# 64-row matmul pairs in the first product of a top-2 expert kernel, with one operand copied to the upper partitions by a DMA

## The chip, the cores and the metric

The kernel runs on one core of one Trainium2 chip. The metric is the device time of one execution in microseconds (us), as the median of several runs. The engines are named as in the profile: PE is TensorE's matmul, PEld its weight load, DVE VectorE, ACT ScalarE, POOL GpSimd, and SP is SyncE, which here only issues DMAs. A "q" behind an engine's name (SPq) means its sequencer.

## What is computed

A causal convolution over the sequence with 7 taps (softmax of a weight per head) makes x of 28672 tokens with 192 columns. Each token goes to the best two of 8 experts, by noisy logits, and the two results are added with their gates:

```python
    logits = x @ w_gate
    noise_scale = np.log1p(np.exp(x @ w_noise))
    noisy_logits = logits + noise_scale * noise
    top2 = np.argpartition(-noisy_logits, 2, axis=1)[:, :2]
    ...
    for e in range(E):
        for k in range(2):
            mask = top2[:, k] == e
            ...
            h = np.maximum(x[mask] @ w1[e], 0.0)
            out[mask] += top2_w[mask, k, None] * (h @ w2[e])
```

D is 192, E is 8, F is 1024; all inputs and the output are float32.

## The kernel before

**Units and rows.** The tokens go through convolution and gating in 28 units of 1024 tokens. `conv` writes a unit's rows as float16 pairs into the tile `rb`: in 384 columns stand the high parts of x's columns 0 to 127, their low parts, and then, together in the third chunk of 128, the 64 high and the 64 low parts of x's columns 128 to 191. `gating(u)` begins by putting loads of noise and a DMA of zeros on SP, then eight DMA transposes of `rb` into `xT` (L475); its later parts compute the logits (L484, with matmuls on `xT`), the top two, the rank of each token (L541, L544) and the row of each token in its expert's region of `xs` in DRAM. POOL scatters the rows there (L570).

**Blocks.** The expert part runs over blocks: rounds of 256 rows (the first round 128), and in each round the experts 0 to 7. That is 232 blocks in order. `load_block` transposes a block's rows out of `xs` into the tile `bT` (L692, by SP; three buffers), with the 384 columns as three chunks of 128 partitions. So chunk 0 holds the high parts of columns 0 to 127, chunk 1 their low parts, and chunk 2 the last 64 columns' high parts on partitions 0 to 63 and their low parts on partitions 64 to 127. The weights are float16 pairs too; the last 64 rows of w1 lie twice, on the lower and on the upper partitions.

**The first product.** `mm1` does half of a block's 1024 hidden columns at a time: four groups `f` of 128 hidden columns into the tile `ph` (two banks, two groups in each), each by five matmuls of 128 rows (L658): weights high and low with chunk 0, weights high with chunk 1, and weights high and low with chunk 2. ACT (L661) and DVE (L662) then make the float16 pair `h` of the half. `mm2` does the second product of 48 matmuls for the block before (L672), ACT scales it (L675), and POOL adds it to the output in DRAM (L676).

**The order.** PE, DVE, ACT and SP execute in the order in which the program issues. Step n of the loop issues: the first half of block n's `mm1`; `prefetch(n + 2)`, which puts the load of block n + 2 on SP; `side.slot(0)`; `mm2` of block n - 1; the second half of block n's `mm1`; `side.slot(1)`. A slot issues pieces of the next units' convolution and gating, as many as a written budget of VectorE time allows, and with them their DMAs: x's load for the next unit (L179) and what `gating` puts on SP. The first units are done ahead of the blocks, in a written order. At the end a loop over overflow rows follows, whose number is computed on the chip.

**Weight scales.** Ahead of the blocks, `gram` (L268) multiplies each expert's weights with themselves, in bfloat16 with 128 columns: per expert 8 matmuls of 128 rows and 8 of 64 rows for w1, and 12 of 128 rows for w2, directly behind each other.

Of the kernel before, what the change touches and what calls it, by code (L numbers as in the profile page):

```python
# [10 lines left out]
F16 = mybir.dt.float16  # L11
# [8 lines left out]
P = 128  # L20
# [12 lines left out]
def kernel(  # L33
# [11 lines left out]
    nc = tc.nc  # L45
# [3 lines left out]
    E, _, F = w1.shape  # L49
# [6 lines left out]
    BIG = 2 * P  # L56
# [4 lines left out]
    rounds = [(0, P)] + [(P + mean * j, mean) for j in range(U)]  # L61
# [24 lines left out]
    start = tc.tile_pool(name="start", bufs=1)  # L86
    spool = start.__enter__()

    xs = dram.tile([E * REG, ROW], F16, name="xs")
# [105 lines left out]
    def parts(e, c):  # L195
        slots, n = ((slots1, 2 * e + c), (slots2, 2 * e + c - 2))[c // 2]
        w = slots[n].bitcast(F16).rearrange("p (a f) -> p a f", a=2)
        return slots[n + 1], w[:, 0], w[:, 1]

    def w1_part(e, c, lo, f):  # L200
        return parts(e, c)[1 + lo][:, f * P:(f + 1) * P]
# [392 lines left out]
    def load_meta(j):  # L594
        start, T = rounds[j]
        mt = ffn.tile([P, E, 2, 8], F32, name="mt", padded_shape=[P, E, 2, 8])
        for h in range(T // P):
            ld = nc.sync.dma_start(
                mt[:, :, h, :],
                dview(xsf, (start + h * P) * ROWF + 192, [[ROWF, P], [REG * ROWF, E], [1, 8]]))  # L600
            loads(ld, j)
        return mt

    def round_meta(j, mt):
        start, T = rounds[j]
        ids, ga = meta(mt, T // P, runs[:, ready[j] + 1, :], float(start))
        if j:
            unscale(ga, slice(0, E), T // P)
        return ids, ga
# [27 lines left out]
    def unscale(ga, es, nh):  # L637
        V.tensor_tensor(ga, ga, winv[:, es, None].to_broadcast([P, es.stop - es.start, nh]), op=OP.mult)
# [3 lines left out]
    def loads(ld, j):  # L642
        for u in scat:
            if u > ready[j]:
                tc.declare_no_dep(ld.ins, group=f"scat{u}", reason="rows behind the block")
            elif u not in waited:
                for s in scat[u]:
                    needs(ld, s)
        waited.update(range(ready[j] + 1))
        tc.add_to_no_dep_group("loads", ld.ins)  # L650

    def mm1(e, xT, T, half, hh, hl):
        nf = FC // 2
        ph = psum.tile([P, nf, BIG], F32, name="ph", bufs=2)
        for f in range(nf):
            seq = [(0, 0, 0), (1, 0, 0), (0, 0, 1), (0, 1, 2), (1, 1, 2)]
            for i, (lo, wc, c) in enumerate(seq):
                nc.tensor.matmul(ph[:, f, :T], w1_part(e, wc, lo, half * nf + f), xT[:, c, :T], start=(i == 0),  # L658
                                 stop=(i == len(seq) - 1))
        hs = slice(half * nf, (half + 1) * nf)  # L660
        halves.append(nc.scalar.activation(hh[:, hs, :T], ph[:, :, :T], AF.Relu))  # L661
        V.scalar_tensor_tensor(hl[:, hs, :T], ph[:, :, :T], 0.0, hh[:, hs, :T], op0=OP.max, op1=OP.subtract)  # L662

    def mm2(j, T, e, hh, hl, ids, gate):
        adds = []
        for h in range(T // P):
            ts = slice(h * P, (h + 1) * P)
            py = psum.tile([P, 512], F32, name="py", bufs=2)
            n = 0
            for f in range(FC):  # L670
                for a, lo in ((hh, 0), (hh, 1), (hl, 0)):
                    nc.tensor.matmul(py[:, :D], a[:, f, ts], w2_part(e, lo, f), start=(n == 0), stop=(n == 3 * FC - 1))  # L672
                    n += 1
            y = ffn.tile([P, D], F32, name="y", bufs=4)
            nc.scalar.activation(y, py[:, :D], AF.Copy, scale=gate[:, h:h + 1])  # L675
            a = nc.gpsimd.indirect_dma_start(  # L676
                out=out, out_offset=bass.IndirectOffsetOnAxis(ap=ids[:, h:h + 1], axis=0),
                in_=y, in_offset=None, compute_op=OP.add)
            for b in adds:
                tc.declare_no_dep(a.ins, b.ins, reason="one expert's rows differ")  # L680
            for u in zeroed:
                if u > ready[j]:
                    tc.declare_no_dep(a.ins, group=f"zeros{u}", reason="rows of tokens not among the block's")
            adds.append(a)
        for a in adds:
            tc.add_to_no_dep_group("adds", a.ins)

    def load_block(j, e):
        start, T = rounds[j]
        xT = ffn.tile([P, 3, BIG], F16, name="bT", bufs=3)  # L690
        r0 = e * REG + start
        ld = nc.sync.dma_start(xT[:, :, :T], xs[r0:r0 + T, 0:384], transpose=True)  # L692
        loads(ld, j)
        return xT


    HH = H // 2
# [44 lines left out]
    ffn = ctx.enter_context(tc.tile_pool(name="ffn", bufs=2))  # L742
# [91 lines left out]
    blocks = [(j, e) for j in range(len(rounds)) for e in range(E)]  # L834
    xTs, metas, mts = {}, {}, {}
# [3 lines left out]
    def prefetch(n):  # L839
        if n < len(blocks) and n not in xTs:  # L840
            j, e = blocks[n]
            side.until(ready[j])
            if e == 0:
                mts[j] = load_meta(j)
            xTs[n] = load_block(j, e)

    for n in range(AHEAD):
        prefetch(n)
    pend = None
    for n, (j, e) in enumerate(blocks):  # L850
        T = rounds[j][1]
        need = max(ready[min(i, len(rounds) - 1)] + j - i for i in range(j, j + 5))
        rate = RATES[min(max(side.gate_done - need, 0), 2)]
        if j not in metas:
            metas[j] = round_meta(j, mts.pop(j))
        ids, gate = metas[j]
        while prepared[0] < e:
            next(prep, None)
        if j == 0:
            unscale(gate[:, e:e + 1, :], slice(e, e + 1), T // P)  # L860
        xT = xTs.pop(n)
        h = ffn.tile([P, 2, FC, BIG], F16, name="h")
        mm1(e, xT, T, 0, h[:, 0], h[:, 1])
        prefetch(n + AHEAD)
        spent = 0.0
        if e == E - 1 and j + 1 < len(rounds):
            metas[j + 1] = round_meta(j + 1, mts.pop(j + 1))
            spent = 1.6
        side.slot(0, T, rate, spent)
        if pend:  # L870
            mm2(*pend)
        mm1(e, xT, T, 1, h[:, 0], h[:, 1])
        side.slot(1, T, rate)
        pend = (j, T, e, h[:, 0], h[:, 1], ids[:, e, :], gate[:, e, :])
# [13 lines left out]
    with tc.If(total > 0):  # L888
        ctr = small.tile([P, 1], F32, name="ctr")
        for e in range(E):  # L890
            nb = nc.values_load(noi[0:1, e:e + 1], engines=engines, min_val=0, max_val=N // P)
            V.memset(ctr, float(cap))
            with tc.For_i(0, nb, 1) as i:
                row = i * P + (e * REG + cap)
                xT = ffn.tile([P, 3, BIG], F16, name="bT", bufs=3)
                nc.sync.dma_start(xT[:, :, :P], xs[bass.ds(row, P), 0:384], transpose=True)
                mt = ffn.tile([P, 1, 1, 8], F32, name="mto")
                nc.sync.dma_start(mt[:, 0, 0, :], xsf[bass.ds(row, P), 192:200])
                es = slice(e, e + 1)
                ids, gate = meta(mt, 1, runs[:, U, es], None, ctr, es)  # L900
                unscale(gate, es, 1)
                V.tensor_scalar(ctr, ctr, float(P), None, op0=OP.add)
                h = ffn.tile([P, 2, FC, BIG], F16, name="h")
                for half in range(2):
                    mm1(e, xT, P, half, h[:, 0], h[:, 1])
                mm2(len(rounds) - 1, P, e, h[:, 0], h[:, 1], ids[:, 0, :], gate[:, 0, :])
# [25 lines left out]
```

## Time and profile before

| | |
|---|---|
| median of 3 runs | 2208.21 us (2207.07 to 2211.52) |
| the profiled execution | 2218.51 us, its span 2216.4 us |
| mean granted TensorE clock | 0.973 |
| PE, DVE, ACT, POOL busy | 93%, 69%, 36%, 60% of the span |
| first product's matmuls (L658) | 9280, of which 8960 with 256 columns and 320 with 128 |
| second product's matmuls (L672) | 10944 |
| loads of blocks (L692) | 232 DMA transposes |
| transposes in gating (L475) | 200 |

The profile is of one execution. Busy times overlap between engines, and matmuls are pipelined: a matmul of 256 columns is listed with 273 ns, while the next one starts earlier; the pace is to be read from the starts. "Idle before" is the time that an engine stood still ahead of an instruction, with what ended it.

### The profile page before, as it was taken

The page shows a single profiled execution, that of the slowest core. Times are in us where ns is not written, and L with a number is a line of the kernel's source. Part 1 is how long each engine was busy: PE and PEld are TensorE (multiplying, and loading weights), DVE is VectorE, ACT ScalarE, POOL GpSimd, SP SyncE. Part 2 cuts the span into 40 slices and gives each one's busy share as a digit, 9 for nine tenths or more (in the row PEclk, how much of TensorE's full clock was granted, in tenths as well). Part 3 has the DMA queues.
Part 4 walks back from the last instruction along what each step waited for, and adds up shares of the span by engine and source line. Part 5 has one row for each costly group of instructions (what it writes and reads, how often), then busy time and mean ns, then how long its engine had stood idle before and what let it go on. Part 6 is the DMA issues. An engine that isn't in the chain of part 4 may idle for free.

```text
span 2216.4 us, 53349 instructions
## 1 busy us (share of the span) xinstructions
PE 2070.0 (93%) x22182; PEld 1929.7 (87%) x22182; DVE 1519.5 (69%) x3975; ACT 795.4 (36%) x1169; POOL 1337.5 (60%) x923
## 2 busy tenths in 40 slices
PE   6768799999999989999999999999999999999997
PEld 5757788888898888899999898999999999999997
DVE  6467777888888877787778777687777874423332
ACT  5254333333333333333333333333333333333332
POOL 0353646766778767667766576557766676543333
PEclk9888999999999999999999999999999999999999
DMA  8523656566666566466655566466665666443332
GB/s 231 170 63 60 140 95 100 97 108 112 120 113 126 109 108 119 73 112 116 117 98 87 105 118 113 70 107 116 117 105 82 112 102 106 74 57 47 50 50 34
DMA packets 462773, 223.65 MB, mean 101 GB/s; under 512 B 342152, under 2 KB 449720, under 8 KB 462393
## 3 DMA queue, kind: packets, MB, share of 16 engines
q1 hardware_dynamic: 375352, 129.38, 29.1%
q0 software_dynamic: 87168, 90.76, 27.2%
q8 instruction: 175, 2.87, 0.5%
q14 instruction: 78, 0.64, 0.1%
HBM read 40.12 MB, written 115.38 MB: 70 GB/s over the span
## 4 chain that ended last, share of the span: by engine, by line
PE 67%; DVE 12%; DMA 4%; issue 4%; SPq 4%; another core or an unknown queue 3%; ACT 3%; POOL 2%; POOLq 0%; DVEq 0%; ACTq 0%
PE ph L658 33%; PE py L672 32%; DVE h L662 3%; SPq L475 3%; DVE xc L415 3%; ACT h L661 2%; POOL out_dram L676 1%; DMA xT<-rb 1%; DMA out_dram<-y,ids 1%; POOL xs L570 1%; PE misc L484 1%; PE ph L391 1%; DVE t L511 0%; DVE w1s L286 0%
## 5 line engine op out<-in xcount | busy, mean ns | idle before, releaser
L676 POOL DMA_INDIRECT out_dram<-y,ids x456 | 805.4, 1766 | 508.5 <-ACT y L675 309.6
L658 PE MATMUL ph<-bT,w1s 128*128 128x256 f16 (+1 forms) x9280 | 1054.4, 272 | 37.6 <-issue 8.5
L658 PEld LDWEIGHTS <-w1s 128*128 128x128 f16 x9280 | 892.8, 98 | 146.3 <-issue 29.2
L672 PE MATMUL py<-w2s,h 128*128 128x192 f16 x10944 | 971.0, 249 | 33.2 <-DVE h L662 23.6
L672 PEld LDWEIGHTS <-h 128*128 128x128 f16 x10944 | 922.3, 99 | 53.8 <-DVE h L662 30.7
L662 DVE SCALAR_TENSOR_TENSOR h<-ph,h 128x1024 f16<-128x1024 f32 (+1 forms) x464 | 557.6, 1202 | 568.4 <-ACT h L661 524.7
L661 ACT ACTIVATE h<-ph 128x1024 f16<-128x1024 f32 (+1 forms) x464 | 466.9, 1008 | 621.0 <-PE ph L658 494.0
L570 POOL DMA_INDIRECT xs<-rb,idx x448 | 513.9, 1147 | 270.9 <-issue 199.5
L415 DVE SCALAR_TENSOR_TENSOR xc<-xt,wt,xc 128x192 f32<-128x192 f32 x1224 | 418.7, 409 | 0.3 <-DMA xt<-zero 0.3
L675 ACT ACTIVATE y<-py,ga 128x192 f32<-128x192 f32 x456 | 190.0, 419 | 619.4 <-PE py L672 451.6
L391 PE MATMUL ph<-xt,dg 128*128 128x192 f32 x224 | 46.0, 375 | 14.0 <-DMA xt<-zero 12.9
L391 PEld LDWEIGHTS ph<-xt,dg 128*128 128x128 f32 x224 | 44.6, 226 | 14.2 <-ACT dg L381 12.8
L413 DVE TENSOR_SCALAR xc<-xt,wt 128x192 f32<-128x192 f32 x204 | 53.0, 323 | 4.4 <-DMA xt<-in_x_dram 4.4
L484 PEld LDWEIGHTS <-xT 128*128 128x128 f16 x1120 | 33.8, 96 | 24.5 <-DMA xT<-rb 23.0
L484 PE MATMUL misc<-ghi,xT 128*128 128x16 f16 x672 | 34.6, 170 | 21.6 <-DMA xT<-rb 20.8
L283 POOL TENSOR_TENSOR w1s<-w1s,w1s 128x1024 f16<-128x1024 f32 x5 | 10.7, 2144 | 69.7 <-ACT w1s L329 69.6
L426 DVE TENSOR_REDUCE am<-xc 128x8 f32<-128x1536 f32 (+1 forms) x27 | 46.4, 1718 | 0.4
L441 DVE TENSOR_TENSOR xc<-xc,xs 128x1536 f32<-128x1536 f32 (+1 forms) x27 | 46.5, 1722 | 0.0
L511 DVE SCALAR_TENSOR_TENSOR t<-t,t 128x64 f32<-128x64 f32 x168 | 40.1, 239 | 5.8
L503 ACT ACTIVATE t<-t 128x64 f32<-128x64 f32 x28 | 7.2, 256 | 98.3 <-DVE t L501 85.3
L446 ACT ACTIVATE rb<-xc 128x1024 f16<-128x1024 f32 x28 | 29.4, 1050 | 17.1 <-DMA xs<-rb,idx 7.2
L449 DVE TENSOR_TENSOR rb<-xc,rb 128x1024 f16<-128x1024 f32 x28 | 34.1, 1216 | 0.8 <-DMA out_dram<-y,ids 0.4
(143 smaller groups left out, 695.4 us busy)
## 6 DMA issues: line engine op xcount, KB each, us to landing
out_dram<-zero SPq DMA_DIRECT2D x28, 768.0 KB
xt<-in_x_dram SPq DMA_DIRECT2D x27, 768.0 KB
out_dram<-y,ids POOLq DMA_INDIRECT x456
xs<-rb,idx POOLq DMA_INDIRECT x448
w2s<-in_moe_w_dram SPq DMA_DIRECT2D x16, 384.0 KB
w1s<-in_moe_w_dram SPq DMA_DIRECT2D x8, 512.0 KB
w1s<-in_moe_w_dram SPq DMA_DIRECT2D x16, 256.0 KB
bT<-xs SPq DMA_TRANSPOSE x232
```

The source lines that it names most:

```text
L391: nc.tensor.matmul(cps[u][-1][1][:, n % nh, :TU * G].rearrange("p (t g) -> p t g", g=G), diag[h, k], xts[u][:, k:k + TU, h * G:(h + 1) * G ...
L413: V.tensor_scalar(dst, src, wt[:, h, k:k + 1], None, op0=OP.mult)
L415: V.scalar_tensor_tensor(dst, src, wt[:, h, k:k + 1], dst, op0=OP.mult, op1=OP.add)
L475: nc.sync.dma_start(xT[:, t], rb[:, t, 0:384], transpose=True)
L484: nc.tensor.matmul(lg[:, t], xT[:, t, c, :], g[:, gc], start=(i == 0), stop=(i == len(seq) - 1))
L570: s = nc.gpsimd.indirect_dma_start(out=xsf, out_offset=bass.IndirectOffsetOnAxis(ap=idx[:, k, t:t + 1], axis=0), in_=rbf[:, t, :], in_offs ...
L658: nc.tensor.matmul(ph[:, f, :T], w1_part(e, wc, lo, half * nf + f), xT[:, c, :T], start=(i == 0), stop=(i == len(seq) - 1))
L661: halves.append(nc.scalar.activation(hh[:, hs, :T], ph[:, :, :T], AF.Relu))
L662: V.scalar_tensor_tensor(hl[:, hs, :T], ph[:, :, :T], 0.0, hh[:, hs, :T], op0=OP.max, op1=OP.subtract)
L672: nc.tensor.matmul(py[:, :D], a[:, f, ts], w2_part(e, lo, f), start=(n == 0), stop=(n == 3 * FC - 1))
L675: nc.scalar.activation(y, py[:, :D], AF.Copy, scale=gate[:, h:h + 1])
L676: a = nc.gpsimd.indirect_dma_start(out=out, out_offset=bass.IndirectOffsetOnAxis(ap=ids[:, h:h + 1], axis=0), in_=y, in_offset=None, compu ...
```

## The change

In `mm1` the matmul of the low part of the weights' last 64 rows (`lo` 1, `wc` 1) no longer reads all 128 partitions of chunk 2. It becomes a matmul of 64 rows, with the high parts of x alone; its product with x's low parts is left out. For two of the four groups of a half it reads partitions 0 to 63 (chunk 2), for the other two partitions 64 to 127, where a new fourth chunk of `bT` holds a copy of the same 64 columns. The four stand one after another, in the order f = 0, 2, 1, 3, so that neighbours use different partitions and different banks. In the first half of a block they come ahead of the 16 matmuls of 128 rows, in the second half behind them. The number of matmuls stays the same. The flags `start` and `stop` are set for the first and last matmul of a bank.

The copy (`upper`) is a DMA on SP from partitions 0 to 63 of chunk 2 to partitions 64 to 127 of chunk 3, 32 KB for a block of 256 rows. That of block 0 is issued before the loop; that of block n + 1 in step n, between the first half of `mm1` and `prefetch(n + 2)`, if the block has been loaded.

```diff
     def mm1(e, xT, T, half, hh, hl):
         nf = FC // 2
         ph = psum.tile([P, nf, BIG], F32, name="ph", bufs=2)
-        for f in range(nf):
-            seq = [(0, 0, 0), (1, 0, 0), (0, 0, 1), (0, 1, 2), (1, 1, 2)]
-            for i, (lo, wc, c) in enumerate(seq):
-                nc.tensor.matmul(ph[:, f, :T], w1_part(e, wc, lo, half * nf + f), xT[:, c, :T], start=(i == 0),
-                                 stop=(i == len(seq) - 1))
+        todo = []
+        for i in range(nf):
+            f, rows = i // 2 + i % 2 * 2, slice(64 * (i % 2), 64 * (i % 2) + 64)
+            todo.append((f, w1_part(e, 1, 1, half * nf + f)[rows], xT[rows, 2 + i % 2, :T]))
+        full = [(f, w1_part(e, wc, lo, half * nf + f), xT[:, c, :T]) for f in range(nf)
+                for lo, wc, c in [(0, 0, 0), (1, 0, 0), (0, 0, 1), (0, 1, 2)]]
+        todo = todo + full if half == 0 else full + todo
+
+        banks = [f // 2 for f, _, _ in todo]
+        for i, (f, w, x) in enumerate(todo):
+            nc.tensor.matmul(ph[:, f, :T], w, x, start=f // 2 not in banks[:i], stop=f // 2 not in banks[i + 1:],
+                             skip_group_check=True)
...
     def load_block(j, e):
         start, T = rounds[j]
-        xT = ffn.tile([P, 3, BIG], F16, name="bT", bufs=3)
+        xT = ffn.tile([P, 4, BIG], F16, name="bT", bufs=3)
         r0 = e * REG + start
-        ld = nc.sync.dma_start(xT[:, :, :T], xs[r0:r0 + T, 0:384], transpose=True)
+        ld = nc.sync.dma_start(xT[:, 0:3, :T], xs[r0:r0 + T, 0:384], transpose=True)
         loads(ld, j)
         return xT
+
+    def upper(xT, T):
+        nc.sync.dma_start(xT[64:P, 3, :T], xT[0:64, 2, :T])
...
     for n in range(AHEAD):
         prefetch(n)
     pend = None
+    upper(xTs[0], rounds[0][1])
     for n, (j, e) in enumerate(blocks):
...
         mm1(e, xT, T, 0, h[:, 0], h[:, 1])
+        if n + 1 in xTs:
+            upper(xTs[n + 1], rounds[blocks[n + 1][0]][1])
         prefetch(n + AHEAD)
```

The loop over overflow rows gets the fourth chunk and the copy too.

More of the change, by code (lines that the diff above doesn't have):

```diff
@@ L894 @@
                 row = i * P + (e * REG + cap)
-                xT = ffn.tile([P, 3, BIG], F16, name="bT", bufs=3)
-                nc.sync.dma_start(xT[:, :, :P], xs[bass.ds(row, P), 0:384], transpose=True)
+                xT = ffn.tile([P, 4, BIG], F16, name="bT", bufs=3)
+                nc.sync.dma_start(xT[:, 0:3, :P], xs[bass.ds(row, P), 0:384], transpose=True)
+                upper(xT, P)
                 mt = ffn.tile([P, 1, 1, 8], F32, name="mto")
```

## The prediction

> **What bounds the kernel now.** I read the page first (shares, slices, costliest groups), then busy time over the stretch of the blocks, then the timeline of PE and of SP around single blocks, then the waits.
>
> ```profile
> span 2216.4 us, 53349 instructions
> PE 2070.0 (93%) x22182; PEld 1929.7 (87%) x22182; DVE 1519.5 (69%) x3975; ACT 795.4 (36%) x1169; POOL 1337.5 (60%) x923
> PE   6768799999999989999999999999999999999997
> DVE  6467777888888877787778777687777874423332
> L672 PE MATMUL py<-w2s,h 128*128 128x192 f16 x10944 | 971.0, 249 | 33.2 <-DVE h L662 23.6 <-issue 6.7 <-ACT h L661 1.9
> L658 PE MATMUL ph<-bT,w1s 128*128 128x256 f16 x8960 | 1029.3, 273 | 12.5 <-issue 8.0 <-DVE xf L136 2.8 <-DVE h L662 0.6
> 188.10:2192.00 2003.90, 1928.75 (x20838) 1798.05 (x20836) 1405.99 (x3641) 703.29 (x1017) 1269.01 (x862) 0.99 0.58 98
> ```
>
> In the window row the columns after the length are PE, PEld, DVE, ACT and POOL busy, then the granted clock. From 188 to 2192 us PE has work in 96% of the time and DVE in 70%: the blocks are bound by the stream of matmuls, so what PE saves or waits there is the kernel's time. 8960 matmuls of 256 columns, 40 to a block, make 224 full blocks; the first 8 blocks have 128 columns.
>
> One block, around 1166 us (the page's slices show the clock full here):
>
> ```profile
> 1162.06 4.12 PE L672 MATMUL py<-w2s,h 128*128 128x192 f16 x48
> 1166.02 4.53 PE L658 MATMUL ph<-bT,w1s 128*128 128x256 f16 x40
> 1171.39 4.12 PE L672 MATMUL py<-w2s,h 128*128 128x192 f16 x48
> ```
>
> Forty matmuls of the first product stand together, the second half of one block (20) and the first half of the next. (4.53 - 0.273)/39 = 0.109 us apart; those of the second product (4.12 - 0.249)/47 = 0.082. A block is 40 x 0.109 + 48 x 0.082 = 8.3 us, and the block whose first half begins inside this row begins at 1166.02 + 20 x 0.109 = 1168.2.
>
> **The change, part by part.**
>
> *The pairs.* Eight of a block's 40 matmuls become 64-row ones, adjacent ones on different rows and different banks. No row of before shows two matmuls on different rows. Bounds for a pair: 0.109 us (a 128-row matmul is two 64-row halves passing together) and 0.218 us (one after the other). I take 0.109, because the 128-row matmul is the nearest row: same rows, same columns, same stream of 256. A full block then saves 4 x 0.109 = 0.436 us; at the other end nothing. TensorE: Matmul & The Clock Gate, Measured speedup vs the span model, in the Trainium skill has the second matmul of such a pack start some 4 ns later; by it 4 x 232 x 4 ns = 4 us would be lost again, and no run here shows it yet.
>
> *Going into 64 rows and back.* This the trace shows: for the weight scales, 8 matmuls of 128 rows, 8 of 64 rows (together the first row) and 12 of 128 rows follow each other without a wait.
>
> ```profile
> 46.81 1.18 PE L268 MATMUL grams<-w1s 128*128 128x128 bf16 x16
> 47.92 0.87 PE L268 MATMUL grams<-w2s 128*128 128x128 bf16 x12
> 48.63 1.18 PE L268 MATMUL grams<-w1s 128*128 128x128 bf16 x16
> 151.11 1.07 PE L658 MATMUL ph<-bT,w1s 128*128 128x128 f16 x16 [0.85 <-DVE w1s L286]
> ```
>
> From 46.81 to 48.63 are 1.82 us for 28 matmuls and one way in and out. Without a change of rows a matmul of 128 columns takes (1.07 - 0.22)/15 = 0.057 (last row) or, within the row of 12, (0.87 - 0.22)/11 = 0.059. In and out cost 1.82 - 28 x 0.057 = 0.22, or 0.17. I take 0.21. TensorEngine Tiling, Key Properties, in the Trainium skill says that a change of the tiling mode drains TensorE; the trace agrees, and these 0.2 us are its price. The order puts the second half's pairs last and the next block's pairs first, so it is one way in and out a block: 224 x (0.436 - 0.21) = 51 us saved. The 8 small blocks save 4 x 0.057 = 0.23 each and pay 0.21: nothing. Where a unit's rank matmuls (128 rows) fall between two blocks, another 0.21 is paid: at most 28 times, 6 us.
>
> ```profile
> L541 PE MATMUL misc<-M,before x28: 189/192/212, 53.8 to 1898.5; 128*128 128x64 f16 x28
> bT<-xs SPq DMA_TRANSPOSE x232
> SPq L692 <- PE ph L658: 766.3, 123, 12.2
> ```
>
> PE's own sum: 45 us saved (bounds +54 if pairs don't overlap, -51 without the rank matmuls).
>
> *The copy's issue.* 232 more DMAs of 32 KB on SP. SP normally sits waiting for PE to free a buffer (last row, 766 us), so 0.4 us of issue more is hidden, and the copy's wait for its load as well: it keeps the next load back, but a load issued when block n begins is needed two blocks later. This cover is gone where SP has other work.
>
> *Where the copy stands in SP's order.* This decides. The copy for block m is issued in step m-1 ahead of that step's load. Everything that step m-2 put on SP after load m goes first, and once per unit that is `gating`: noise, zeros, and eight transposes of `rb`.
>
> ```profile
> 1153.80 0.34 SPq L179 DMA_DIRECT2D xt<-in_x_dram  x1
> 1154.24 1.21 SPq L692 DMA_TRANSPOSE bT<-xs  x1
> 1155.50 0.59 SPq L366 DMA_DIRECT2D out_dram<-zero  x1
> 1156.14 13.74 SPq L475 DMA_TRANSPOSE xT<-rb  x8
> 1169.98 2.56 SPq L692 DMA_TRANSPOSE bT<-xs  x2
> L475 SPq DMA_TRANSPOSE xT<-rb x200: 1249/1267/4175, 266.1 to 1869.3; - x100
> ```
>
> The load at 1154.24 is that of the block that begins at 1168.2. Its copy can't be issued before 1169.9, when the eighth transpose is out: 1.7 us after PE needs it, since the pairs are the first matmuls of the block. Before, SP's lateness hurt nobody, because loads run two blocks ahead; the copy runs only one ahead. 200 transposes are 25 such groups. Here are the first after the start (SP; the block begins 13 matmuls into the PE row, at 332.0), and the last (block at 1870.04 + 2.2 = 1872.3):
>
> ```profile
> 320.52 13.51 SPq L475 DMA_TRANSPOSE xT<-rb  x8
> 330.58 3.76 PE L658 MATMUL ph<-bT,w1s 128*128 128x256 f16 x33 [0.36 <-issue]
> 1857.76 12.81 SPq L475 DMA_TRANSPOSE xT<-rb  x8
> 1870.04 4.63 PE L658 MATMUL ph<-bT,w1s 128*128 128x256 f16 x40
> ```
>
> They end 2.0 after and 1.7 before the block's start. In 20 units nothing else stands before the copy, and read so, the end lies -1.8 to 3.7 us after the block's start, 1.7 on average. To this come 0.1 us of gap on SP, the copy's flight, and 0.4 because PE reaches the block two shorter blocks earlier while the transposes don't get faster. For the flight the nearest row is the unit at 1085 us:
>
> ```profile
> 1085.16 13.66 SPq L475 DMA_TRANSPOSE xT<-rb  x8
> 1100.47 0.18 PE L484 MATMUL misc<-ghi,xT 128*128 128x16 f16 x1 [1.46 <-DMA xT<-rb]
> PE misc L484 <- DMA xT<-rb: 20.8, 14, 7.2
> ```
>
> The last transposes were out at 1098.82 and PE got them at 1100.47: 1.65 us after the issue ends, 2.9 after it begins (1.27 each). A copy's issue is shorter, 0.34 as x's load above: between 0.34 + 1.65 = 2.0 and 2.9; I take 2.5. So PE waits 1.7 + 0.1 + 2.5 + 0.4 = 4.7 us, 20 times: 94. In four units x's load stands between group and copy; they wait 0 to 3 us, 5 together. In the unit of the 266 us group PE waits for these transposes anyway; 1 us more. PE's present waits for xT later in the same block go: 20.8 less the start's, 10. Sum: 94 + 5 + 1 - 10 = 90 us (flight's ends: +-11).
>
> *The clock after a wait.* Three windows, one before and two after the wait of 1.46 us above, then one around a wait of 4.7 us that ended at 195.15:
>
> ```profile
> 1091.00:1095.60 4.60, 4.60 (x53) 4.38 (x51) 4.60 (x13) 0.84 (x2) 3.69 (x4) 1.00 1.29 181
> 1100.70:1104.10 3.40, 3.40 (x26) 3.23 (x23) 3.40 (x11) 0.26 (x1) 2.92 (x2) 0.51 1.13 160
> 1104.10:1107.50 3.40, 3.40 (x40) 3.27 (x38) 2.23 (x7) 0.84 (x2) 3.10 (x2) 1.00 0.03 2
> 192.70:199.50 6.80, 4.35 (x35) 4.07 (x35) 3.29 (x14) 0.21 (x1) 0.00 (x0) 0.50 0.01 2
> ```
>
> After the wait 3.4 us pass at half clock, 1.7 us lost; after the longer one 4.35, 2.2 lost. With 1.9 for each of 22 new waits over 1.5 us, less the four places where the trace has this loss already (after 1100, 1243, 1386 and 1458 us, 1.7 each): 42 - 7 = 35 us (bounds -7 without any, +48 at 2.5). The Trainium skill (TensorE: Matmul & The Clock Gate, HAM oscillation) names idle gaps over some 3.4 us as the ones that lower the clock; the trace lowers it after 1.5 us, and by the rule four of my waits, those of 2 to 3.2 us, would be free, 8 us less.
>
> *Sum.* -45 + 90 + 35 = +80 on the profiled execution's 2218.5 us: 2298. That execution lies 10 us above the median of 2208.2; against the median it is 2288.
>
> **The rivals.**
> 1. *SP is through sooner: faster.* Place: the group of eight transposes. It takes 13.5 us where 8 x 1.27 = 10.2 would do. That isn't a wait for `rb`, which DVE had done seven microseconds ahead of the group at 1156:
>
> ```profile
> 1148.37 0.68 DVE L451 TENSOR_TENSOR rb<-xc,rb 128x512 f16<-128x512 f32 x1
> ```
>
>    So the transfers in front (x's load, the zeros) hold the issue up. If a slower pace of blocks thins them out and all 3.3 us go, a wait is 4.7 - 3.3 = 1.4 us, too short for the clock: 2208 - 45 + 20 x 1.4 + 6 - 10 = 2187. It decides from the point where a wait with its clock loss is under 2 us (22 x 2 = 45). Against it: the same transfers are issued in the same order, close before the group.
> 2. *Pairs don't overlap.* +54 in place of -45, and PE, 0.4 us later after two blocks instead of 0.4 earlier, waits 22 x 0.85 = 19 less: 2208 + 54 + 71 + 35 = 2368. No row excludes it.
> 3. *The clock isn't lowered:* 2288 - 35 = 2253. The windows speak against it.
>
> **How the numbers follow.** Forecast 0.70; rivals 0.08, 0.11, 0.08; 0.03 for no change, somewhere between rival 1 and the forecast. The time is the forecast's, 2288. The range runs from the forecast without the clock's loss and with the flight at 2.0 us (2288 - 35 - 11), less a third of the group's 3.3 us in 20 units by rival 1's cause, 2225, to the forecast with the flight at 2.9 and the clock's loss at 2.5 a wait, plus a third of the pairs' bound, 2345; rivals 1 and 2 lie outside. 0.2% (about what a measurement of this kernel can tell) is 4.4 us: slower 0.89, same 0.03, faster 0.08.
>
> **What the profile after would show.** If right: first-product matmuls of 64 rows whose pairs start 0.109 us apart, with some 0.1 us more at each change of rows; a new wait of PE's first matmul of a block on the copy, some 22 times, 3 to 7 us long, each just after a group of eight transposes on SP; more slices of half clock; the waits of L484 on xT gone or smaller; elsewhere blocks of 8.1 us. The prediction is wrong if pairs stand 0.218 us apart, if the copy's issue comes ahead of the transposes, or if the waits on the copy sum to under 45 us.

## The result, and the profile after

The changed kernel takes 2301.65 us (2286.91 to 2312.64, 4 runs); the kernel before beside it takes 2209.86 us (2207.07 to 2213.27). The ratio is 1.041 (95% interval 1.0345 to 1.0476): 4% slower. The profiled execution of the changed kernel took 2296.5 us, its span is 2294.6 us.

The page, PE's waits and SP's waits of the changed kernel (lines have moved: the first product is L668, its ACT and DVE parts are L671 and L672, the second product is L682, the load L702, the copy L707):

```profile
PE 2057.2 (90%) x22182; PEld 1810.6 (79%) x22182; DVE 1521.7 (66%) x3975; ACT 795.0 (35%) x1169; POOL 1307.5 (57%) x923
PE   6768689989898999998899899998899899999998
PE ph L668 27%; PE py L682 23%; SPq L475 11%; DVE h L672 7%; DVE xc L415 4%; ACT h L671 3%; DMA bT<-bT 2%; DVE xc L413 1%; DVE t L511 1%; PE misc L484 1%; DMA w1s<-in_moe_w_dram 1%; DMA w2s<-in_moe_w_dram 1%; DMA xt<-in_x_dram 1%; DVE oh L523 0%
...
PE ph L668 <- DMA bT<-bT: 105.0, 30, 19.8
PE py L682 <- issue: 12.6, 32, 1.0
PE ph L668 <- issue: 11.2, 24, 1.1
...
SPq L702 <- PE ph L668: 520.4, 126, 10.1
SPq L707 <- DMA bT<-xs: 310.5, 141, 5.5
```

PE now idles 105 us in front of the first product for the copy (`bT<-bT`), in 30 waits; the longest, 19.8 us, is in the unit in which SP also has eight DMAs of zeros into `xs` ahead of its group of transposes. The eight transposes of gating (L475, on SP) carry 11% of the chain that ended last. No wait of L484 on `xT` of any size is left; before they were 20.8 us. SP waits 310 us for loads to land ahead of a copy; before it spent this time waiting for PE.

One unit, SP first, then PE, then busy time around PE's wait (the clock stands behind the five engines):

```profile
1117.92 1.38 SPq L702 DMA_TRANSPOSE bT<-xs  x1
1119.35 0.57 SPq L365 DMA_DIRECT2D nzt<-in_moe_noise_dram  x1
1119.98 0.49 SPq L366 DMA_DIRECT2D out_dram<-zero  x1
1120.56 13.24 SPq L475 DMA_TRANSPOSE xT<-rb  x8
1133.84 0.59 SPq L707 DMA_DIRECT2D bT<-bT  x1
...
1131.78 0.48 PE L668 MATMUL ph<-bT,w1s 64*128 64x256 f16 x5 [0.25 <-issue]
1136.76 4.11 PE L668 MATMUL ph<-bT,w1s 64*128 64x256 f16 x19 [4.50 <-DMA bT<-bT]
...
1136.80:1140.20 3.40, 3.40 (x17) 2.18 (x17) 0.00 (x0) 0.00 (x0) 0.00 (x0) 0.50 0.40 83
1140.20:1140.90 0.70, 0.70 (x11) 0.53 (x9) 0.00 (x0) 0.00 (x0) 0.00 (x0) 0.50 0.15 23
```

At 1131.8 PE runs the four 64-row matmuls that end a block and the first one of the next; the second one needs the copy. SP is at the seventh transpose then, ends the eighth at 1133.8, issues the copy, and PE goes on at 1136.76, 2.9 us after the copy's issue began. The next 4.1 us run at half clock.

Where no convolution or gating runs beside the blocks (the last 300 us), the first product's group of 40 matmuls in the changed kernel, to be held against the 4.53 us of before:

```profile
2053.83 4.12 PE L682 MATMUL py<-w2s,h 128*128 128x192 f16 x48
2057.79 4.31 PE L668 MATMUL ph<-bT,w1s 128*128 128x256 f16 x40
```

### The profile page after: what moved, and what is told of

Same layout as the page of the kernel before. It is cut to its first block, busy times and chain, and to the rows that moved or that the text cites. A ratio compares the mean times of both kernels' runs of the same rounds, so it can differ in the third digit from the quotient of the medians.

```text
span 2294.6 us, 53668 instructions
## 1 busy us (share of the span) xinstructions
PE 2057.2 (90%) x22182; PEld 1810.6 (79%) x22182; DVE 1521.7 (66%) x3975; ACT 795.0 (35%) x1169; POOL 1307.5 (57%) x923
## 4 chain that ended last, share of the span: by engine, by line
PE 52%; DVE 20%; SPq 12%; DMA 5%; issue 4%; ACT 4%; another core or an unknown queue 1%; POOL 0%; DVEq 0%; POOLq 0%; ACTq 0%
PE ph L668 27%; PE py L682 23%; SPq L475 11%; DVE h L672 7%; DVE xc L415 4%; ACT h L671 3%; DMA bT<-bT 2%; DVE xc L413 1%; DVE t L511 1%; PE misc L484 1%; DMA w1s<-in_moe_w_dram 1%; DMA w2s<-in_moe_w_dram 1%; DMA xt<-in_x_dram 1%; DVE oh L523 0%
## 5 line engine op out<-in xcount | busy, mean ns | idle before, releaser
L668 PE MATMUL ph<-bT,w1s 128*128 128x256 f16 (+3 forms) x9280 | 1042.7, 277 | 142.4 <-DMA bT<-bT 105.0
L668 PEld LDWEIGHTS <-w1s 128*128 128x128 f16 (+1 forms) x9280 | 782.3, 99 | 347.1 <-issue 241.4
L682 PE MATMUL py<-w2s,h 128*128 128x192 f16 x10944 | 973.4, 248 | 41.1 <-DVE h L672 21.8
L672 DVE SCALAR_TENSOR_TENSOR h<-ph,h 128x1024 f16<-128x1024 f32 (+1 forms) x464 | 557.5, 1202 | 668.4 <-ACT h L671 616.4
L682 PEld LDWEIGHTS <-h 128*128 128x128 f16 x10944 | 916.4, 99 | 70.0 <-DVE h L672 30.4
L671 ACT ACTIVATE h<-ph 128x1024 f16<-128x1024 f32 (+1 forms) x464 | 466.8, 1008 | 731.3 <-PE ph L668 621.7
L570 POOL DMA_INDIRECT xs<-rb,idx x448 | 484.7, 1082 | 337.2 <-issue 200.5
L484 PEld LDWEIGHTS <-xT 128*128 128x128 f16 x1120 | 34.3, 100 | 2.5 <-ACT xT L467 0.5
L484 PE MATMUL misc<-ghi,xT 128*128 128x16 f16 x672 | 33.0, 172 | 0.4 <-ACT xT L467 0.4
L484 PE MATMUL misc<-glo,xT 128*128 128x16 f16 x448 | 32.3, 171 | 0.0
```

The costliest lines, as they stand in the source:

```text
L484: nc.tensor.matmul(lg[:, t], xT[:, t, c, :], g[:, gc], start=(i == 0), stop=(i == len(seq) - 1))
L570: s = nc.gpsimd.indirect_dma_start(out=xsf, out_offset=bass.IndirectOffsetOnAxis(ap=idx[:, k, t:t + 1], axis=0), in_=rbf[:, t, :], in_offs ...
L668: nc.tensor.matmul(ph[:, f, :T], w, x, start=f // 2 not in banks[:i], stop=f // 2 not in banks[i + 1:], skip_group_check=True)
```

## Experiments

All ratios are to the kernel before, run on the same chip in the same comparison. There were three comparisons. In the second the kernel before took 2144.9 us, in the others 2213 to 2214 us, so times of different comparisons aren't held against each other, ratios only with care. "Issue stalls" are PE's stops that end by issue, that is, by nothing that the profile shows. The waits list counts idle time from the modelled end of a matmul; where I give one sum for a kernel, it is counted from the starts of matmuls, over the blocks from the ninth on, as what a start comes later than the stream's pace, outside half-clock windows, stops over 0.15 us: 27 us in the trace of the kernel before shown above, which was taken ahead of the three comparisons.

**The pairs without the copy.**

```diff
-            todo.append((f, w1_part(e, 1, 1, half * nf + f)[rows], xT[rows, 2 + i % 2, :T]))
+            todo.append((f, w1_part(e, 1, 1, half * nf + f)[rows], xT[rows, 2, :T]))
...
-        nc.sync.dma_start(xT[64:P, 3, :T], xT[0:64, 2, :T])
+        pass
```

> The pairs of the change without the copy: the upper rows read chunk 2's own upper partitions (x's low parts in place of the high ones), and no copy is issued. Theory (the matmul order saves 45 us, the late copy costs it): 2210 - 45 = 2165 us, no wait of PE at a block's start, clock as before (mean 0.97). Rival (the 64-row matmuls themselves are slow, or lower the clock): 2250 or more.

Measured: 2213.33 us, ratio 1.0003 (0.997 to 1.0037). The rival's number isn't met, but neither is mine: the pairs alone gain nothing. Busy time (PE first, number of matmuls in brackets) before and in this kernel, in two stretches with convolution and gating beside the blocks and in one without:

```profile
600.00:1200.00 600.00, 578.05 (x6315) 537.57 (x6313) 476.31 (x1291) 214.09 (x313) 414.62 (x278) 0.99 0.61 107
1200.00:1900.00 700.00, 684.19 (x7483) 642.28 (x7482) 512.30 (x1338) 252.97 (x367) 463.08 (x320) 0.99 0.61 103
1900.00:2160.00 260.00, 258.73 (x2732) 244.02 (x2730) 84.07 (x127) 89.44 (x124) 112.82 (x78) 1.00 0.40 56
```

```profile
600.00:1200.00 600.00, 568.34 (x6257) 499.88 (x6254) 472.23 (x1274) 211.34 (x309) 417.47 (x279) 0.98 0.63 106
1200.00:1900.00 700.00, 678.28 (x7526) 598.59 (x7522) 518.72 (x1356) 253.63 (x369) 465.45 (x321) 1.00 0.60 103
1910.00:2170.00 260.00, 258.89 (x2809) 233.55 (x2809) 84.27 (x108) 91.74 (x128) 115.98 (x80) 1.00 0.42 57
...
PE py L682 <- issue: 22.2, 42, 1.7
PE ph L668 <- issue: 20.8, 51, 1.1
```

Without that other work the blocks run 2.8% faster (2809 matmuls against 2732 in 260 us). Beside it there are 13783 matmuls against 13798 in 1300 us: no gain. The stream is shorter there too, but PE stops by issue 93 times where it stopped 37 times (8.5 us, 24 times, and 6.7 us, 13 times); counted from starts 63 us against 27.

**The copy issued by ACT.**

```diff
-        nc.sync.dma_start(xT[64:P, 3, :T], xT[0:64, 2, :T])
+        nc.scalar.dma_start(xT[64:P, 3, :T], xT[0:64, 2, :T])
```

> The change with the copy issued by ACT in the same place of the program, so that it doesn't stand behind SP's eight transposes. Theory (SP's order makes the copy late): the waits on the copy fall from 105 us to under 20, 2165 to 2185 us. Rival (the copy is slow in the transfers themselves, behind x's load and the zeros, whoever issues it): the waits stay over 60 us, 2250 us or more.

Measured: 2229.67 us, ratio 1.0074 (1.0045 to 1.0103). PE's waits on the copy:

```profile
PE ph L668 <- DMA bT<-bT: 14.5, 13, 3.2
```

So the wait was SP's order: the same copy at the same place of the program, on another queue, costs 14.5 us of waits instead of 105, and the transfers aren't what made it late. The time lies above my range, 2165 to 2185 us, by about as much as that of the pairs alone lies above mine for them.

**The copy unread.** The first product of before, and the copy issued as in the change.

> The copy of the change, issued where it is, with the 128-row matmuls of before, so that nothing reads it. Theory (issue and traffic of 232 copies are hidden, only the wait of the pairs costs): 2210 us, within 6 of before. Rival (the copies' own time on SP or their traffic delays the loads): 2230 us or more, with new waits of PE on the loads.

Measured: 2229.48 us, ratio 1.0063 (1.0027 to 1.0099), 14 us. My "within 6" is wrong, the rival's 2230 nearly met. PE's waits of this kernel; before, the three were 8.5, 6.7 and 3.5 us:

```profile
PE ph L659 <- issue: 17.3, 37, 1.5
PE py L673 <- issue: 12.5, 31, 1.0
...
PE ph L659 <- DMA bT<-xs: 8.8, 4, 3.4
```

The copies cost something though nobody waits for them: 5 us of waits on loads, as the rival has it, and more issue stalls, 48 us from starts.

**64-row matmuls, not paired.**

```diff
-            f, rows = i // 2 + i % 2 * 2, slice(64 * (i % 2), 64 * (i % 2) + 64)
-            todo.append((f, w1_part(e, 1, 1, half * nf + f)[rows], xT[rows, 2 + i % 2, :T]))
+            f, rows = i // 2 + i % 2 * 2, slice(0, 64)
+            todo.append((f, w1_part(e, 1, 1, half * nf + f)[rows], xT[rows, 2, :T]))
...
-        nc.sync.dma_start(xT[64:P, 3, :T], xT[0:64, 2, :T])
+        pass
```

> All 64-row matmuls on partitions 0 to 63, without a copy, in the same order: the ways in and out of 64 rows stay, the overlap goes. The product is the change's own. Theory (a 64-row matmul alone takes 0.109 us, in and out 0.21 a block): 2210 + 54 = 2264 us. Rival (the ways in and out are hidden or cheaper at 256 columns): 2210 to 2235 us.

Measured: 2258.41 us, ratio 1.0181 (1.012 to 1.0242), 45 us over before, where 54 were expected. Its group of 40:

```profile
2050.41 4.74 PE L668 MATMUL ph<-bT,w1s 128*128 128x256 f16 x40
```

4.74 - 4.53 = 0.21 us is the way into 64 rows and back, as taken from the weight scales at 128 columns (single 64-row matmuls start 0.109 us apart here, like those of 128 rows). And 4.74 - 4.31 = 0.43 us is what four pairs save against eight single matmuls: the pairs overlap fully. In the changed kernel's last 300 us the second matmul of a pair starts 3 to 5 ns after the first, and the next pair 105 to 117 ns later.

The second comparison (the kernel before at 2144.85 us, 2136.52 to 2156.59) was to move the copy, and to find what stops PE.

**The eight transposes in two groups of four.** `gating` yields after four, and the other four go out one block later:

```diff
             for t in range(TU):
+                if t == TU // 2:
+                    yield 0.0
                 nc.sync.dma_start(xT[:, t], rb[:, t, 0:384], transpose=True)
...
```

The rest of the edit, left out here, makes the slots resume `gating` one block later.

> The change, with gating's eight transposes put on SP in two groups of four, one block apart, so that the copy stands behind four of them; the same DMAs in all. Theory (the place in SP's order makes the copy late): the waits on the copy fall from 105 us to under 30, and the time to that of the copy issued by ACT, 2215 to 2235 us. Rival (SP has too much to issue per unit, wherever the copy stands): waits over 60 us, 2260 us or more.

Measured: 2187.13 us, ratio 1.0202 (1.016 to 1.0244).

```profile
PE misc L486 <- DMA xT<-rb: 37.8, 41, 2.9
PE ph L670 <- DMA bT<-bT: 27.8, 16, 13.3
```

The waits on the copy fell below 30 us, 13.3 of them one wait at the first group. But the second four now land too late for the logits: 37.8 us of waits on `xT`. The place of the copy is confirmed; as a repair it moves the wait on, and the ratio lies between that of the change, 1.041, and that of the copy issued by ACT, 1.0074.

**The copy right behind its load.**

```diff
         loads(ld, j)
+        nc.sync.dma_start(xT[64:P, 3, :T], xT[0:64, 2, :T])
         return xT

     def upper(xT, T):
-        nc.sync.dma_start(xT[64:P, 3, :T], xT[0:64, 2, :T])
+        pass
...
```

> The copy issued right behind its own load, two blocks ahead of its use. Theory (place in SP's order): no copy stands behind the eight transposes of its own block any more, but SP now waits some 3.5 us for each load to land, and the load and copy behind the group come later by that: waits of 0 to 4 us a unit, 20 to 60 us in all, 2230 to 2265 us. Rival (any wait on SP for a landing is hidden two blocks ahead): waits under 15 us, 2215 to 2230 us.

Measured: 2214.13 us, ratio 1.0316 (1.0272 to 1.036). SP in one unit, and PE's waits:

```profile
1132.03 1.32 SPq L702 DMA_TRANSPOSE bT<-xs  x1
1137.30 0.47 SPq L704 DMA_DIRECT2D bT<-bT  x1
...
1138.51 12.31 SPq L475 DMA_TRANSPOSE xT<-rb  x8
...
PE misc L484 <- DMA xT<-rb: 76.8, 59, 10.7
PE ph L668 <- DMA bT<-bT: 9.9, 9, 1.5
```

The copy is in time (9.9 us). But SP stands from 1133.4 to 1137.3 for the load, the eight transposes start that much later, and PE waits 76.8 us for them. I had the price too low, a ratio of 1.03 where my range of 2230 to 2265 us means 1.01 to 1.025, and the victim wrong: I looked at the next block's load and copy, and it was the group itself.

**Without the zeros: the pairs, and the kernel before.** The zeros are the largest transfer that gating starts.

```diff
-        zi = nc.sync.dma_start(dview(out, u * TU * D, [[I * D, P], [D, TU], [1, D]]),
+        if u < 3:
+            zi = nc.sync.dma_start(dview(out, u * TU * D, [[I * D, P], [D, TU], [1, D]]),
...
```

> The pairs without the copy (as in the first run), and without the zeros that gating writes to the output (768 KB a unit) from the fourth unit on; so the sums start from what lies in the output. Theory (the pairs' 45 us went into stalls of PE that end by issue, 63 us against 27 before, and these come from the DMA traffic beside the blocks): issue stalls under 40 us, 30 us or more faster than before without the zeros. Rival (the stalls don't come from this traffic): issue stalls stay over 50 us, within 12 us of before without the zeros.

> The kernel before, without the zeros from the fourth unit on. Theory (traffic makes the issue stalls): 10 to 20 us under before, issue stalls under 15 us. Rival: issue stalls stay at some 27 us, and only the shorter wait for xT shows, 0 to 12 us under before.

Measured: the pairs 2114.87 us, ratio 0.9856 (0.9807 to 0.9906); before without zeros 2133.46 us, ratio 0.9944 (0.9924 to 0.9964): the pairs are 19 us faster here. Neither trace has an issue stall from the ninth block on. But the two kernels above, in the same comparison and with their zeros, have none either. So the zeros alone don't make the issue stalls, and this pair of runs doesn't tell my theory from its rival. It does tell that without issue stalls (and without the zeros) the pairs gain, though 19 us and not 45. PE's waits in the pairs' kernel and in the one before:

```profile
PE misc L542 <- DVE M L537: 15.2, 21, 5.0
PE py L683 <- ACT h L672: 5.7, 2, 3.3
PE ph L669 <- DVE xf L136: 8.0, 1, 8.0
```

```profile
PE misc L542 <- DVE M L537: 8.1, 5, 3.3
PE ph L659 <- DMA bT<-xs: 9.4, 2, 6.1
```

The rank matmuls now wait for DVE in 21 units instead of 5: part of what PE saves it spends waiting for an engine that doesn't get faster. Counted from starts, the waits on DVE and ACT grow from 25 to 46 us.

The third comparison (the kernel before at 2213.11 us, 2202.62 to 2233.51) repeats the two main kernels and moves ACT's copy ahead of the first half.

```diff
+        if n + 1 in xTs:
+            upper(xTs[n + 1], rounds[blocks[n + 1][0]][1])
         mm1(e, xT, T, 0, h[:, 0], h[:, 1])
-        if n + 1 in xTs:
-            upper(xTs[n + 1], rounds[blocks[n + 1][0]][1])
```

> The changed kernel as it is, once more beside the kernel before, since PE's stalls that end by issue were 27 us and more in the first four comparisons and none in the second four. Theory (the late copy costs PE's waits and the clock, wherever the issue stalls come from): 3 to 4.5% slower, waits on the copy 90 us or more, with or without issue stalls. Rival (the loss hangs on the chip's stalls): under 2%.

> The pairs without the copy again (upper rows read x's low parts). Theory (the pairs save 45 us of PE's stream, and only the issue stalls ate it): without issue stalls 30 to 45 us under before (ratio 0.979 to 0.986); with issue stalls like in the first comparison 0.995 to 1.005. Rival (something in the pairs eats the gain): 1.000 without issue stalls too.

> The change with the copy issued by ACT, again. Theory: without issue stalls 15 to 40 us under before (ratio 0.982 to 0.993), 5 to 15 us above the run without the copy; with issue stalls 1.007 as before. Rival (the copy costs on ACT as much as on SP): 1.01 or more.

> The copy issued by ACT at the start of the step, ahead of the first half's activation instead of behind it, some 4 us earlier. Theory (what is left of the wait is the copy's lateness): its waits fall from some 15 us to under 5, and the time to that without the copy, within 6 us. Rival (ACT now waits for late loads, and PE's halves behind it): 5 us or more over the copy behind the activation.

| kernel | us | ratio (95% interval) | waits on the copy, us | issue stalls from starts, us |
|---|---|---|---|---|
| the change again | 2301.03 | 1.040 (1.0361 to 1.0438) | 100.0 | 38 |
| pairs without the copy again | 2207.39 | 0.9978 (0.9952 to 1.0003) | none | 56 |
| copy by ACT again | 2228.53 | 1.006 (1.0031 to 1.0089) | 23.4 | 60 |
| copy by ACT, earlier | 2254.27 | 1.0184 (1.0154 to 1.0214) | 6.2 | 88 |

(The waits on the copy are of the waits list.)

The issue stalls were there again, so with the zeros in place the pairs and the copy by ACT weren't seen without them. The first three repeat. The earlier copy brings the waits down to 6.2 us, about as I said, and is 26 us slower all the same, as the rival has it. Whether the reason is ACT's waits for late loads isn't shown: what grew in PE's waits is issue stalls, and DVE's h (24.0 us against 18.8).

No version tried here with the zeros in place beats the kernel before beyond its interval.

## Why the prediction was right, point by point

The predicted 2288 us and the measured 2302 agree, and so does the main term; but two steps, tested alone, were wrong, and one agreement is in part luck.

*The pairs, and the way into 64 rows and back.* Right, on the nearest rows: 0.43 us for four pairs (0.436 taken), 0.21 for in and out. Counted from starts over the blocks from the ninth on, the matmuls' stream is 90 us shorter, and the ways cost 47 (57 taken): 43 us less, where the sum has 45. Of the 4 us that the later start of a pair's second matmul might cost, nothing shows: behind the first step of 0.12 us, which the unpaired 64-row matmuls have as well, pairs follow each other 0.109 to 0.110 us apart.

*The copy behind the eight transposes.* Right in its place, and in its sum, but not unit by unit. The sum had 100 us of waits less 10 for `xT`; measured are 105 us, less 20.4 of waits on `xT`, so 85 against 90. Of the 105, however, 19.8 fall in the unit that has the zeros into `xs` on SP too. Before, PE waited 12.0 us for `xT` there, and the sum had 1 us more; it was 8. The other 29 waits are 85 us, where the sum had 99: those over 1.5 us are 22, as forecast, but 3.6 us long on average, not 4.7. That these two errors partly cancel is luck. The flight was 2.9 us in the unit shown, my upper end, not 2.5.

*The clock.* Right in kind: the windows above show 4.1 us at half clock behind such a wait. From starts, half-clock windows cost 47 us, 21 before: 26, where I took 35. Not every wait pays it: half clock follows, within 1.4 us, on 18 of those 22 waits, on one of 1.89 us (ended at 1885.2) but not on one of 3.21 us (ended at 1511.4). So the length of the wait alone doesn't decide.

*"What PE saves or waits there is the kernel's time."* This step failed for the saving. PE busy in 96% of the stretch says nothing of what comes next when the stream gets shorter. The pairs alone are worth 0 and 6 us in two comparisons, with intervals that include none, and 19 in the one without issue stalls. The saving is in the stream. Where there are issue stalls, most of it comes back as these (27 to 63 and 56 us); where there are none, about half of it as waits on DVE and ACT (25 to 46 us).

*"0.4 us of issue more is hidden, and the copy's wait for its load as well."* Failed by 14 us, the unread copy's price. The step from the pairs alone to the copy by ACT, 16 and 21 us, is no second measure of it, since it has 14.5 and 23.4 us of PE's waits on the copy in it.

*The sum.* It can be split in two ways. Taken inside the changed kernel's own trace, against the trace of before, the stream is 43 us shorter, the waits on the copy and on `xT` are 85 us more, half clock 26 and issue stalls 4 (31 against 27): 72 of the 78 us by which the spans differ. My terms were -45, 90, 35 and 0, so they are there, each near its size. Taken by removing one part after the other, with the repeats, the pairs give -6, the copy issued by ACT some 21 on top of them, and its place behind the transposes 2301 - 2229 = 72: 88 us together. The two ways differ because PE's stops stand in for each other: the pairs alone have 63 and 56 us of issue stalls, the copy by ACT 74 and 60, the change only 31 and 38, while PE stands for the copy instead. Why they give way like this isn't shown; an experiment for it alone wasn't made. So the forecast of the change holds by its terms, but the saving among them can't be had by taking the late copy away, which its sum would have promised. (The lower end of the range, redone, is 2288 - 35 - 11 - 22 = 2220, not 2225.)

*The rivals.* "SP is through sooner" is out: the group takes 13.24 us in the unit shown, 13.5 taken. Its 1.4 us of wait wouldn't have been too short for the clock either: in the kernel before, a wait of 1.33 us that ended at 1386.0 has half clock from 1387.4 to 1390.8 behind it. That transfers in front hold the group up is borne out in part: the median group takes 13.3 us in the kernel before and 11.0 without the zeros, though in another comparison (12.3 us there for the copy behind its load, with zeros). "Pairs don't overlap" is out by 4.31 against 4.74 us. "The clock isn't lowered" is out by the windows.

## What to carry to other kernels

Before a DMA is added to a queue, list what the program puts on that queue between the data's arrival and its use: here one group of eight transposes, 13 us long, stood in a distance of two blocks for the load (harmless) and of one block for the copy (22 waits of 3.6 us on average, and one of 19.8). A saving in the engine that is busy 96% isn't yet the kernel's: take the pace from a stretch where little else runs, and then look at how the engine's stops behave in the stretches where much runs. And a wait on another queue doesn't vanish by moving it: behind its load the copy made the transposes late, on ACT it was cheap only at one of two places.

## What the runs showed of the hardware that I had not expected

PE has stops that end by no semaphore that the profile shows. Weight loads of the kernel without the copy, in one such series:

```profile
1363.52 0.33 PEld L682 LDWEIGHTS <-h 128*128 128x128 f16 x4 [0.35 <-issue]
...
1364.28 0.41 PEld L668 LDWEIGHTS <-w1s 128*128 128x128 f16 x4 [0.35 <-issue]
1365.02 0.33 PEld L668 LDWEIGHTS <-w1s 128*128 128x128 f16 x4 [0.34 <-issue]
1365.76 0.42 PEld L668 LDWEIGHTS <-w1s 128*128 128x128 f16 x4 [0.41 <-issue]
...
1363.50:1366.50 3.00, 2.49 (x18) 1.49 (x17) 0.66 (x2) 0.42 (x1) 1.94 (x3) 1.00 0.19 68
```

PE gets through four weight loads with their matmuls every 0.74 us, where the pace is 4 x 0.109 = 0.44, while the 16 DMA engines are 19% busy and the clock is full. In the first and third comparison, and in the two traces ahead of them, such stops sum to 27 us or more in every kernel profiled. In the second all four kernels had next to none, and there the kernel before was 3% faster, 68 us. That isn't the stops alone: the four kernels reached their ninth block at 164 to 171 us there, the others at 175 to 188. Nor is it the chip, since the first two comparisons ran on the same one. And the stops aren't scattered by chance. The pairs without the copy were traced twice, on two chips; with PE's stream cut into stretches of 44 matmuls, 78% of the second trace's issue stalls lie in the 12% of stretches in which the first trace has some. The zeros alone don't make them. They grew when PE's stream got shorter (27 to 63 us), but also with the unread copy (48 us), where it didn't. What makes them stays open; so does what the changed kernel would lose without them.
